# Larger first loads in a fused attention and Fourier-mix kernel: two head pairs in one transfer, and every engine's order made anew

## The chip, the cores and the metric

The kernel runs on one core of a Trainium2 chip. The metric is the device time of one execution in microseconds. The engines are TensorE (PE, with its weight loads PEld), VectorE (DVE), ScalarE (ACT), GpSimd (POOL) and SyncE (SP). DMA transfers are issued by SP and ACT on hardware queues, and by POOL on one software queue.

## The reference

Four batches, eight heads, 768 tokens, 64 values per head; d_model is 512. First a local attention with a linear distance bias, then a two-dimensional Fourier mix and a feed-forward part:

```python
scores = scale * np.matmul(q, k.transpose(0, 1, 3, 2))
keep = is_global | is_local          # 8 global keys, a band of 96
scores = np.where(keep, scores - slopes * dist, -1e9)
x = softmax(scores) @ v              # heads side by side: (4, 768, 512)
X = np.fft.fft(np.fft.fft(x, axis=1), axis=2)
u = x + np.real(X)
un = (u - mean(u)) / np.sqrt(var(u) + 1e-6)
out = u + np.maximum(un @ w_ch1, 0.0) @ w_ch2
```

All inputs and the output are float32; the kernel casts to float16 as it loads.

## The kernel before

Heads are taken in pairs (pair 0 holds heads 0 and 1, and so on to pair 3). The work is cut into units in four lists. In the unit names below, the number counts along the list.

- A, attention. For a pair of the first two batches: a unit that transposes q and k on TensorE (line 599), three score units (lines 676 and 690, with the exponential on ScalarE at line 713) and the products with v (line 769). Batch 0: A0 and A1 transpose pair 0, A2 to A4 are its scores, A5 transposes pair 2, A6 pair 1, A7 to A9 are scores of pair 2, A12 to A14 of pair 1, A15 transposes pair 3, A18 to A20 are its scores; A10 and A11, A16 and A17, A21 and A22, A23 and A24 are the two halves of the products with v of pairs 0, 2, 1 and 3. Batch 1: A25, A26, A30 and A34 transpose its pairs, A27 to A29, A31 to A33 and so on are scores, A41 to A44 products with v.
- M, the mix. Batch 0: M0 and M1 fold the output of pairs 1 and 3 on TensorE (line 960; pairs 0 and 2 are folded on VectorE, lines 913 to 945), M2, M3, M9 and M10 are the first transform (line 1052), M4 to M6 spread x (line 1113), M7, M8 and M13 the second transform (line 1140), M11, M12 and M14 transpose the centred rows.
- H, the first feed-forward product (line 1287), eight units for each of twelve chunks of 256 rows.
- G, the second feed-forward product (lines 1320 and 1429).

Every unit leaves follow-up operations for the other engines, named unit.number: the copy of transposed q and k out of PSUM (line 623 on VectorE, line 626 on ScalarE), the copy of a part of the transposed keys (lines 630 and 631; the scores need it), the exponentials, the normalization (lines 779 and 781), and so on. Loads, table work and the copies of v (lines 740 and 742; the products with v need them) have names that begin with T.

The order on each engine is written out by hand in the table `ORDER` of the class `Plan`: five lists of such names, one for each engine. The code only replays them (`run`, `unit_start`, `op_start`, `op_go`); engines wait for each other by semaphores. The constants in `op_go` and `move` are a cost model of the transfers; they choose among operations that are ready and free buffers, while each engine's own order is the list's. POOL's list holds its transfers among its copies, so a copy stands behind the transfers ahead of it. A software transfer takes one of eight lanes (`self.soft`), and must wait until the transfer that holds the lane has landed.

The loads of batch 0: pair 0's q and k come as four float32 transfers on the hardware queues (line 515) and are cast by ScalarE and VectorE. For pairs 1 to 3, POOL issues one transfer for q and one for k of each pair (line 539), and two for each pair's v (line 482; 64 partitions each). The table of distances for the scores (`misc<-distm`, line 1554) is also issued by POOL, behind q and k of pairs 2 and 3. Batch 1 already loads some pairs together: `n == 4` in `load_qk` (line 530) takes q of two pairs in one transfer, and `load_v` takes v by four heads (line 476).

Of the kernel before, what the change touches and what calls it, by code (L numbers as in the profile page):

```python
# [17 lines left out]
class Ring(str):  # L18

    k = 0  # L20
    n = 1
# [3 lines left out]
class Plan:  # L25
# [85 lines left out]
    def op_go(self, eng, name, start):  # L111
# [2 lines left out]
        fn()  # L114
        end = self.t[eng] = start + cost
        if dma:
            at = max(max(end + 0.55, 4.9) if eng == "POOL" else end + lat + 2.7 * (lat == 1.0 and end > 3.5), self.now)
            cell = [self.NEVER]
            self.q["SW" if eng == "POOL" else "AQ" if eng == "ACT" and at < 6.5 else "HW"].append([at, *dma, outs, uses, cell])
            lanes = self.lanes if nd > 0 else self.soft  # L120
            for _ in range(abs(nd)):
                lanes.append(cell)
                lanes.pop(0)
            if then is not None:
                self.tok[then] = end
            return
# [50 lines left out]
    def unit_start(self, unit):  # L177
# [7 lines left out]
        if not there:  # L185
# [6 lines left out]
    EQ = 4  # L192
    AQ = ()
    HW = (0,)
    U0 = 2
    PZ = 15
    EARLY = ("qk2", "qk1", "v0", "v2", "qk3", "v1", "v3")
    ORDER = {
# [9 lines left out]
        ),  # L208
        "ACT": (
# [9 lines left out]
        ),  # L219
        "DVE": (  # L220
# [11 lines left out]
        ),  # L232
        "POOL": (
# [5 lines left out]
        ),  # L239
        "SP": (  # L240
            "T.6 T.0 T.136 T.35 T.10 T.127 T.133 T.128 T.130 T.134 T.91 G7.1 G3.1 T.137 T.131 T.100 T.101 T.176 T.185 T.205 T.102 T.177 T.206 T.182 T.34 "
            "T.140 T.186 T.211 T.212 T.183 T.149 T.179 T.180 T.150 T.151 T.223 T.189 T.222 T.229 T.228 T.198 T.199 T.239 T.200 T.240 T.246 T.245 T.256 "
            "T.258 T.257 "
        ),
    }

# [60 lines left out]
def kernel(  # L307
# [85 lines left out]
    pl = Plan()  # L393
# [60 lines left out]
    stage = {}  # L454
# [10 lines left out]
    def load_v(b, hp):  # L465
        h0 = 2 * hp
        if b >= FB:
# [2 lines left out]
                                    v[b, h0:h0 + 2].rearrange("h (i m) d -> m (h i) d", m=P))  # L470
            swq(whole, 1.08, [("avdone", b - 2), ("wl", 7)], [("v", b, hp, t) for t in range(2)], (1536, 0.93), False)
            return
        if b == 1:
            for t in range(2 - hp % 2 * 2):
                def four(t=t):
                    nc.gpsimd.dma_start(v16[b % 2][64 * t:64 * t + 64, h0:h0 + 4, :, 0:Dh].rearrange("m h i d -> m (h i) d"),
                                        v[b, h0:h0 + 4].rearrange("h (i m t) d -> t m (h i) d", m=64, t=2)[t])
                swq(four, 1.08, [], [("v", b, hp, t), ("v", b, hp + 1, t)], (1536, 0.93))
            return
# [9 lines left out]
    def load_qk(b, hp):  # L489
# [3 lines left out]
        for w, src in enumerate((q, k)):  # L493
# [9 lines left out]
            def place():  # L503
                if (tag, ti) not in stage:
                    stage[tag, ti] = buf(tag, ti, [P, 2 if n < 6 else 1, 2, 2, NP, 2, Dh], FP16, 2 if n < 6 else 1)
                qk16[n] = stage[tag, ti][:, :, n % 2] if tag == "tt" else stage[tag, ti][:, n % 2 if n < 6 else 0]
            rows = src[b, h0:h0 + 2].rearrange("h s d -> (h s) d").rearrange("(m p t) d -> p m (t d)", p=P, t=2)
            if n in pl.HW:
                for h in range(2):
# [13 lines left out]
                             [("qk", n, w, h)], [("free", "u", w + n)], rank=0)  # L523
                continue

            if n == 4:
                def two(w=w, src=src):
                    place()
                    qk16[n + 1] = stage[tag, ti][:, :, 1]
# [1 line left out]
                                        src[b, h0:h0 + 4].rearrange("h s d -> (h s) d").rearrange("(m p t) d -> p m (t d)", p=P, t=2))  # L531
                swq(two, 1.08, free(tag, ti), [("qk", n, w), ("qk", n + 1, w)], (1536, 1.53))
                continue
            if n == 5:
                continue

            def run(w=w, rows=rows):
# [1192 lines left out]
```

## Time and profile before

| | |
|---|---|
| runs shown | 251.08, 251.26 (median), 252.32 us |
| profiled execution | 251.96 us, span of its instructions 250.2 us |
| mean granted TensorE clock | 0.986 |
| bytes | HBM read 31.48 MB, written 8.65 MB |

A row of busy time by stretches gives the stretch, then for each engine its busy time and number of instructions, the clock that was granted to TensorE (1.00 is full), the DMA share and the rate. A timeline row gives start, length, engine, line, operation, the tiles (out<-in), and in brackets how long the engine had been idle before it and what ended that. The sum of 1.76 us around the span belongs to the execution and not to any instruction.

### The profile page before, as it was taken

To read this page: it belongs to the slowest core of one execution; us is meant where nothing else is said; L and a number is where in the kernel's file an instruction comes from. 1 tells how busy PE (TensorE), PEld (TensorE's weight loads), DVE (VectorE), ACT (ScalarE), POOL (GpSimd) and SP (SyncE) were. 2 spreads that over 40 slices of the span, in tenths; PEclk is the share of its full clock that TensorE was granted. 3 is DMA by queue.
4 is the path that set the end of the run, shared out by engine and by line. 5 is a ranking of instruction groups with operands and counts; after the bars stand their busy time and mean duration, and the time that the engine had idled before them with its cause. 6 is when DMAs were issued, how large, how long until landed. Compare 5 with 4: busy or idle time off the path is not lost.

```text
span 250.2 us, 7615 instructions
## 1 busy us (share of the span) xinstructions
PE 235.1 (94%) x3251; PEld 193.0 (77%) x3251; DVE 199.0 (80%) x430; ACT 132.9 (53%) x222; POOL 111.1 (44%) x157
## 2 busy tenths in 40 slices
PE   7668799899999999999899999999999999999993
PEld 2446596778766667797788888899889888988882
DVE  1368999668988449999989999899996695676682
ACT  3038458886354698975276766825536353503300
POOL 8789928999570108997009412550004010300110
PEclk9979799999999999999999999999999999999999
DMA  7999999999999899999999780941913332032022
GB/s 156 204 139 135 213 195 203 186 125 177 163 135 196 208 190 86 193 133 107 252 240 244 48 107 5 156 35 35 245 61 125 47 105 65 1 86 84 3 84 84
DMA packets 96017, 32.88 MB, mean 131 GB/s; under 512 B 84304, under 2 KB 92624, under 8 KB 95984
## 3 DMA queue, kind: packets, MB, share of 16 engines
q0 software_dynamic: 66256, 17.39, 69.3%
q1 hardware_dynamic: 26416, 12.23, 24.4%
q10 hardware_dynamic: 3312, 2.79, 4.2%
q8 instruction: 25, 0.41, 0.7%
q14 instruction: 8, 0.07, 0.1%
HBM read 31.48 MB, written 8.65 MB: 160 GB/s over the span
## 4 chain that ended last, share of the span: by engine, by line
PE 79%; DMA 6%; DVE 6%; ACT 3%; POOL 2%; issue 1%; ACTq 0%; POOLq 0%
PE ph L1287 34%; PE pgD L1429 13%; PE pgA L1429 10%; PE pg L1320 6%; PE pav L769 4%; DMA misc<-distm 3%; PE py L1052 3%; DMA unT<-un 3%; PE pu L1140 3%; PE sc L684 3%; ACT ex L713 2%; PE sc L676 2%; POOL hT L539 1%; PE sc L690 1%; DVE qkT L623 1%
## 5 line engine op out<-in xcount | busy, mean ns | idle before, releaser
L1287 PE MATMUL ph<-unT,w 128*128 128x256 f16 x768 | 95.0, 273 | 1.0 <-DMA unT<-un 1.0
L1287 PEld LDWEIGHTS <-w 128*128 128x128 f16 x768 | 73.2, 98 | 12.3 <-DMA unT<-un 1.1
L1293 ACT ACTIVATE hT<-ph 128x512 f16<-128x512 f32 x74 | 43.3, 596 | 65.8 <-PE ph L1287 65.6
L1233 POOL TENSOR_SCALAR sm<-sm 128x2 f32<-128x2 f32 x12 | 4.0, 336 | 76.7 <-ACT un L1226 76.3
L1429 PEld LDWEIGHTS <-hT 128*128 128x128 f16 x320 | 30.8, 98 | 4.3 <-issue 0.4
L713 ACT ACTIVATE ex<-sc 128x1024 f16<-128x1024 f32 (+1 forms) x24 | 21.9, 957 | 13.8 <-PE sc L690 13.5
L710 ACT ACTIVATE er<-sc 128x1024 f16<-128x1024 f32 (+1 forms) x24 | 22.5, 952 | 10.2 <-PE sc L684 8.3
L1447 DVE SCALAR_TENSOR_TENSOR u<-pgA,sm,u 128x256 f32<-128x256 f32 (+1 forms) x30 | 17.1, 570 | 6.9 <-PE pgA L1429 6.6
L1294 DVE TENSOR_SCALAR hT<-ph 128x512 f16<-128x512 f32 x22 | 15.1, 688 | 6.7 <-PE ph L1287 6.5
L725 DVE TENSOR_TENSOR ex<-er,mk 128x1024 f16<-128x1024 f16 (+1 forms) x24 | 16.2, 686 | 4.4 <-ACT er L710 4.4
L1447 DVE SCALAR_TENSOR_TENSOR u<-pgD,sm,u 128x512 f32<-128x512 f32 (+1 forms) x21 | 15.2, 723 | 4.3 <-PE pgD L1429 4.0
L1320 PE MATMUL pg<-w,hT 128*128 128x512 f16 x64 | 15.8, 379 | 0.0
L769 PEld LDWEIGHTS <-ex 128*128 128x128 f16 x352 | 13.3, 99 | 2.1 <-issue 1.3
L1226 ACT ACTIVATE un<-un 128x512 f16<-128x512 f16 x24 | 14.9, 622 | 0.0
L1304 POOL DMA_INDIRECT out_dram<-u,back x4 | 4.7, 1184 | 22.3 <-DVE u L1447 22.0
L499 POOL DMA_DIRECT2D qk<-in_q_dram x16 | 13.3, 847 | 2.5 <-DMA w<-in_moe_w_ch_dram 1.4
L769 PE MATMUL pav<-v,ex 128*128 128x65 f16 x224 | 13.9, 196 | 0.1
L499 POOL DMA_DIRECT2D qk<-in_k_dram x16 | 13.4, 846 | 0.0
L676 PE MATMUL sc<-misc 64*64 64x512 f16 (+1 forms) x96 | 10.8, 422 | 2.8 <-DMA misc<-distm 1.2
L781 DVE TENSOR_TENSOR x<-pav,rc 128x384 f16<-128x384 f32 x24 | 12.6, 554 | 0.6
L1217 ACT ACTIVATE un<-u,sm 128x512 f16<-128x512 f32 x17 | 11.9, 714 | 1.7 <-DVE sm L1184 1.7
L623 DVE COPY qkT<-pt 128x1536 f16<-128x1536 f16 (+1 forms) x8 | 6.6, 850 | 6.8 <-PE pt L599 6.8
(170 smaller groups left out, 492.6 us busy)
## 6 DMA issues: line engine op xcount, KB each, us to landing
w<-in_moe_w_ch_dram POOLq DMA_DIRECT2D x8, 512.0 KB, 8.2
out_dram<-u SPq DMA_DIRECT2D x15, 256.0 KB, 2.5
v<-in_v_dram POOLq DMA_DIRECT2D x12, 192.0 KB, 5.8
qk<-in_q_dram POOLq DMA_DIRECT2D x16, 96.0 KB, 6.2
qk<-in_k_dram POOLq DMA_DIRECT2D x16, 96.0 KB, 5.0
xr<-xd SPq DMA_DIRECT2D x3, 512.0 KB, 4.3
xd<-x ACTq DMA_DIRECT2D x2, 768.0 KB, 4.4
v<-in_v_dram POOLq DMA_DIRECT2D x8, 96.0 KB, 7.6
```

The costliest lines, as they stand in the source:

```text
L499: nc.gpsimd.dma_start(qk16[n][:, w, :, h], src[b, h0 + h].rearrange("(i m) d -> m i d", m=P))
L676: nc.tensor.matmul(o, sid[r, 2 * hp + s, r], m, start=True, stop=False, skip_group_check=True, tile_position=(64 * s, 64 * t))
L710: A(mine(), cut(pa), AF.Exp, 0.0, 0.125)
L713: A(cut(expst[hp][:, :, g * 512:g * 512 + (384 if g == 2 else 512)]), cut(pa), AF.Exp, 0.0, 0.125)
L725: VT(o, mine(), m, op=ALU.mult)
L769: nc.tensor.matmul(o[:, s * 65:(s + 1) * 65], lhsT, w, start=(a == 0), stop=(a == len(ops) - 1), skip_group_check=True)
L1287: nc.tensor.matmul(ph[:, a * CH:(a + 1) * CH].rearrange("p (x m) -> p x m", x=2), W1[0][:, d, jb * P:(jb + 1) * P], UNT[c][:, :, d, :], st ...
L1293: pl.later([("ACT", act(512), lambda: A(dst, ph, AF.Relu)), ("DVE", dve(512), lambda: V.tensor_scalar_max(dst, ph, 0.0))], [], e, [("h", c ...
L1294: ("DVE", dve(512), lambda: V.tensor_scalar_max(dst, ph, 0.0))],
L1320: nc.tensor.matmul(pg, HT[c][:, jb, t * P:(t + 1) * P], W2[0][:, jb, :], start=(jb == 0), stop=(jb == NJ - 1))
L1429: nc.tensor.matmul(o, lhs(j), rhs(j), start=(first and j == 0), stop=(j == NK - 1), skip_group_check=True)
L1447: V.scalar_tensor_tensor(o, x, r(t), acc, op0=ALU.mult, op1=ALU.add)
```

## The change

Batch 0's pairs 2 and 3 are loaded together: q of four heads in one transfer, k of four heads in another, and v by four heads in two transfers instead of four. POOL issues 10 loads for batch 0's q, k and v instead of 14. The constant that the cost model gives for the start of the first software transfer goes from 4.9 to 5.5, and the lists of all engines are other ones.

```diff
-            at = max(max(end + 0.55, 4.9) if eng == "POOL" else end + lat + 2.7 * (lat == 1.0 and end > 3.5), self.now)
+            at = max(max(end + 0.55, 5.5) if eng == "POOL" else end + lat + 2.7 * (lat == 1.0 and end > 3.5), self.now)
...
     HW = (0,)
+    PAIRS = (2, 3)
...
-        if b == 1:
+        if b == 1 or hp in pl.PAIRS:
             for t in range(2 - hp % 2 * 2):
...
-                qk16[n] = stage[tag, ti][:, :, n % 2] if tag == "tt" else stage[tag, ti][:, n % 2 if n < 6 else 0]
+                qk16[n] = stage[tag, ti][:, :, n % 2] if n in (4, 5) or n in pl.PAIRS else stage[tag, ti][:, n % 2 if n < 6 else 0]
...
-            if n == 4:
+            if n in (4,) + pl.PAIRS[:1]:
...
-            if n == 5:
+            if n in (5,) + pl.PAIRS[1:]:
                 continue
```

The lists, by what differs at their heads (before, then after; the T numbers shift, since there are fewer loads):

```diff
 PE
-A0 A5 A1 A15 A3 A2 A4 A7 A20 A6 A9 A8 A10 A19 A11 A12 A14 A30 A16 A13 A17 A18 A21 A22 A37 A36 A23 M0 A24 A25 A34 M1 M4 A35 A26 A28 A38 M5 M2
-A29 A39 M3 M9 A32 M7 A40 M8 A31 M10 M6 A27 M11 M13 H0 A33 H1 A43 H2
+A0 A1 A3 A5 A15 A2 A6 A9 A4 A7 A8 A10 A18 A11 A14 A16 A12 A13 A17 A30 A20 A21 A19 A22 A25 A26 A23 A34 A24 A37 M0 M1 A38 A35 M5 A36 A39 M2 M3
+A28 M4 M7 A29 M8 M9 M6 M11 M10 A27 A40 H0 A33 A32 H1 M13 H2 A31 H3
...
 ACT (its two or three transfers first; A1.1, A1.2, A15.1, A6.1 are copies out of q and k)
-T.2 T.8 T.4 T.7 T.1 T.5 A3.0 A4.0 A2.0 A7.0 A20.0 A8.0 A19.0 A9.0 A14.0
+T.0 T.4 T.9 T.1 T.5 A1.1 A1.2 A3.0 A15.1 A2.0 A6.1 A4.0 A9.0 A8.0 A7.0 A14.0
...
 DVE (A6.0 is pair 1's key copy, T.66 before and T.62 after pair 0's copy of v)
-T.53 T.51 T.3 A1.1 A1.2 T.49 A5.1 A15.1 T.52 A15.0 T.66 A6.1 T.50 A6.0 A10.0 A11.0 T.68
+T.7 T.45 T.3 T.47 A5.1 A6.0 T.62 T.48 T.46 T.64 A10.0 A11.0 T.66
...
 POOL (A1.0 and A5.0 are key copies of pairs 0 and 2; T.9 before is the distance table, T.26 after is q of batch 1's third pair)
-T.11 T.12 T.19 T.20 T.9 T.14 T.15 T.16 T.18 T.13 T.17 T.21 T.22 A1.0
+T.11 T.12 T.13 T.14 T.15 T.18 T.16 T.17 T.26 A1.0 T.21 T.20 A5.0
```

In the new lists the distance table (T.9) is the third transfer that ScalarE issues; the identity goes to SyncE. From the fourth chunk on the lists of all engines differ in many places by one to three entries.

More of the change, by code (lines that the diff above doesn't have):

```diff
@@ L199 @@
         "PE": (
[8 rows of a table removed]
[8 rows of a table added]
         ),
         "ACT": (
[9 rows of a table removed]
[9 rows of a table added]
         ),
         "DVE": (
[11 rows of a table removed]
[11 rows of a table added]
         ),
         "POOL": (
[5 rows of a table removed]
[5 rows of a table added]
         ),
         "SP": (
-            "T.6 T.0 T.136 T.35 T.10 T.127 T.133 T.128 T.130 T.134 T.91 G7.1 G3.1 T.137 T.131 T.100 T.101 T.176 T.185 T.205 T.102 T.177 T.206 T.182 T.34 "
-            "T.140 T.186 T.211 T.212 T.183 T.149 T.179 T.180 T.150 T.151 T.223 T.189 T.222 T.229 T.228 T.198 T.199 T.239 T.200 T.240 T.246 T.245 T.256 "
-            "T.258 T.257 "
+            "T.8 T.6 T.2 T.129 T.123 T.31 T.132 T.124 T.126 T.130 T.87 T.133 T.10 T.127 G7.1 G3.1 T.96 T.97 T.172 T.98 T.173 T.30 T.181 T.178 T.201 T.136 "
+            "T.202 T.182 T.208 T.207 T.175 T.179 T.145 T.176 T.146 T.218 T.147 T.224 T.219 T.185 T.194 T.225 T.195 T.196 T.242 T.236 T.235 T.241 T.252 "
+            "T.254 T.253 "
         ),
```

66 rows, old and new, of the table ORDER are left out of this document.

## The prediction

> **What bounds the kernel now.** I read the page first, then busy time by stretches, then the timelines of single engines in the first 55 us, at last the chain that ended last.
>
> ```profile
> span 250.2 us, 7615 instructions
> PE 235.1 (94%) x3251; PEld 193.0 (77%) x3251; DVE 199.0 (80%) x430; ACT 132.9 (53%) x222; POOL 111.1 (44%) x157
> ...
> 0.00:20.00 20.00, 13.80 (x211) 8.52 (x212) 7.74 (x19) 6.49 (x9) 16.23 (x29) 0.91 1.72 167
> 20.00:40.00 20.00, 17.51 (x427) 14.44 (x427) 18.92 (x51) 13.06 (x18) 14.82 (x22) 0.91 1.55 186
> 40.00:60.00 20.00, 19.00 (x381) 14.73 (x374) 15.77 (x38) 16.75 (x28) 19.01 (x31) 1.00 1.45 168
> ...
> 100.00:120.00 20.00, 18.65 (x332) 15.49 (x330) 19.76 (x42) 14.77 (x25) 17.08 (x21) 1.00 1.92 148
> ...
> 15.00:20.00 5.00, 4.73 (x118) 3.73 (x119) 2.30 (x4) 3.63 (x5) 4.94 (x11) 0.67 2.41 141
> 25.00:30.00 5.00, 3.24 (x77) 2.64 (x74) 4.85 (x12) 2.92 (x3) 4.80 (x8) 0.85 1.69 213
> 30.00:35.00 5.00, 5.00 (x116) 4.30 (x115) 4.44 (x20) 2.27 (x5) 3.01 (x5) 0.81 1.45 184
> ```
>
> Columns: the stretch, busy PE, PEld, DVE, ACT, POOL with counts, granted clock, DMA share, GB/s. PE is idle for 15.1 us of the span: 6.2 in the first 20 us, 2.5 in the next, 1.0 up to 60, 1.35 between 100 and 120, the rest in the tail. So from the first feed-forward product on PE is the bound, and time can come only from the 9.7 us idle before it, from 1.35 us later, and from the reduced clock: busy time times (1 - clock) is 1.6, 0.5 and 0.95 us in the last three rows, 3.0 in all. From 20 to 40 us DVE is busy for 18.92 of 20: there DVE carries the chain, and PE fills.
>
> The first load waits, on POOL, PE and ACT:
>
> ```profile
> 8.49 0.75 POOL L482 DMA_DIRECT2D v<-in_v_dram  x1 [0.77 <-DMA hT<-in_q_dram]
> 9.58 0.83 POOL L539 DMA_DIRECT2D hT<-in_q_dram  x1 [0.34 <-DMA hT<-in_k_dram]
> 10.68 0.75 POOL L482 DMA_DIRECT2D v<-in_v_dram  x1 [0.28 <-DMA hT<-in_q_dram]
> 11.76 0.74 POOL L482 DMA_DIRECT2D v<-in_v_dram  x1 [0.33 <-DMA hT<-in_k_dram]
> 13.36 0.74 POOL L482 DMA_DIRECT2D v<-in_v_dram  x1 [0.86 <-DMA misc<-distm]
> 14.10 0.71 POOL L630 COPY mk<-qkT 128x512 f16<-128x512 f16 x1
> 14.87 0.29 POOL L631 COPY mk<-qkT 128x128 f16<-128x128 f16 x1
> 15.21 0.31 PE L690 MATMUL sc<-qkT,mk 64*64 64x128 f16 x2 [1.54 <-POOL mk L631]
> 9.34 1.63 PE L599 MATMUL pt<-ident,hT 128*64 128x128 f16 x36 [0.56 <-DMA hT<-in_k_dram]
> L626 ACT ACTIVATE qkT<-pt 128x1536 f16<-128x1536 f16 x1 | 1.4, 1444 | 0.0
> L713 ACT ACTIVATE ex<-sc 128x1024 f16<-128x1024 f32 x16 | 16.1, 1024 | 11.3 <-PE sc L690 11.0
> ```
>
> POOL has eight loads under way; the ninth waits until the first has landed. The releases 8.49, 9.58, 10.68, 11.76 are q2, k2, q3, k3 of the first batch: 1.09 us for 192 KB, and 13.36 the distance table, 1.60 us. Pair 0's scores wait for its key copy on POOL, at 14.10.
>
> **The change, part by part.** *Loads.* q2 and q3 become one transfer, k2 and k3 another. The queue moves a load in 1.09 us however many wait, so merging saves no queue time: the merged q lands when k2 did, 9.4, the merged k when k3 did, 11.7. Pair 2 loses 1.1 us on q and 2.2 on k. The table leaves POOL's queue for ACT's, where it runs beside these loads: that costs them 0 to 1.6 us (its price in the old queue); I take 1.1, since the hardware queue moves it at the same time as the other: q at 10.5, k at 12.8. Later loads come 1.6 less 1.1 earlier. POOL issues four loads fewer (0.75 to 0.83 each), and four of the rest carry twice the bytes; it waits for landings there, so this is worth nothing by itself.
>
> The Trainium skill (DMA: Bandwidth & Descriptors, Anatomy of one DMA) gives each such transfer about 2.0 us of fixed time besides its bytes. By that, four transfers fewer would save 8 us. The spacing of 1.09 us shows that in this queue the fixed part lies under the neighbours, and the trace decides.
>
> *First score.* The new order has eight loads, then the ninth (q of batch 1's third pair), then pair 0's key copy. So POOL waits to 10.5, issues (0.83), copies (1.05 from the rows at 14.10 and 14.87): the first score starts at 12.4, not 15.21. The transposes of pair 0 end by 8, so PE idles from 8 to 12.4 and begins at half clock. Score, pair 2's and pair 3's transposes (24 each; 36 took 1.63 at full clock) then take about 0.9, 1.4 and 1.2: 15.9. Before, the same five units were done at 16.0. Nothing is won yet.
>
> *Copies out.* Four copies of transposed q and k go from DVE to ACT. ACT, in order: pair 3's copy from 15.9 (1.44), an exponential (1.02), pair 1's copy (1.44): 19.8. DVE's next entry is pair 1's key copy, which waits for that; then comes pair 0's v copy. So DVE starts its long stretch at 20.5, and not at 15.85:
>
> ```profile
> 15.85 0.53 DVE L740 COPY vB<-v 128x528 f16<-128x528 f16 x1 [0.99 <-DMA v<-in_v_dram]
> ...
> 19.60 0.96 DVE L623 COPY qkT<-pt 128x1536 f16<-128x1536 f16 x1 [1.80 <-PE pt L599]
> ...
> 20.80 0.82 DVE L630 COPY mk<-qkT 128x512 f16<-128x512 f16 x1
> 21.66 0.50 DVE L631 COPY mk<-qkT 128x128 f16<-128x128 f16 x1
> 22.32 0.20 DVE L779 RECIPROCAL rc<-pav 128x6 f32<-128x6 f32 x1 [0.17 <-PE pav L769]
> ...
> 29.42 0.28 DVE L630 COPY mk<-qkT 128x512 f16<-128x512 f16 x1
> ...
> 34.53 0.20 DVE L779 RECIPROCAL rc<-pav 128x6 f32<-128x6 f32 x1 [0.42 <-PE pav L769]
> ...
> 35.24 0.68 DVE L965 CAST zy<-pf 128x512 f16<-128x512 f32 x1
> ...
> 44.18 0.68 DVE L1068 CAST zy<-py 128x512 f16<-128x512 f32 x1
> 47.48 0.69 DVE L1068 CAST zy<-py 128x512 f16<-128x512 f32 x1 [1.69 <-ACT zy L1066]
> ...
> 53.36 1.03 PE L1287 MATMUL ph<-unT,w 128*128 128x256 f16 x8
> ```
>
> Before, DVE goes from 15.85 to 44.18, when the fold is done: 28.3 us. In the new order this stretch loses the idle 1.80, 0.17 and 0.42, one copy out (0.96), a key copy (1.3 of 20.80 to 22.16), another (0.55 at 29.42) and a cast (0.68): 5.9. It gains a key copy (0.55) and two scalings (0.4). So 23.4 us from 20.5: 43.9, 0.3 earlier. This supposes that PE always has the next piece ready.
>
> *From the fold to the first feed-forward product, H0.* 9.2 us now. DVE's wait of 1.69 at 47.48 goes, since that cast now stands behind the sums of M7; two casts come to DVE (0.69, and one of 128x1024, about 1.2 from 0.69 for half of it); the transposes M11 stand right behind M6 instead of after A27. I follow the new order: M3 and its casts 46, M7 47.3, its sums 49.1, centring on ACT 50.7, M11 51.2, copied out 51.9. H0 starts at 51.95, 1.4 earlier.
>
> *What PE still owes at H0.* A31, A32 and M13 stood ahead of H0 and come after it now:
>
> ```profile
> 49.67 0.41 PE L676 MATMUL sc<-misc 64*64 64x512 f16 x4
> 50.24 0.39 PE L1052 MATMUL py<-t,ww 128*128 128x256 f16 x2
> 52.46 1.00 PE pu L1140 x16
> ```
>
> A score is 0.57 (start to next start), M13 1.0: 2.1 us. As PE is full from there, they are paid in full: -1.4 + 2.1 = +0.7.
>
> *Later.* One stall can go:
>
> ```profile
> PE ph L1287 <- DMA unT<-un: 1.0, 1, 1.0
> 112.29 7.66 DMA unT<-un
> 32.34 1.79 PE pf L960 x32
> ```
>
> The centring that this transpose waits for stands two H units earlier in the new order. That is worth 0 to 1.35 us (all idle of 100 to 120), if nothing takes its place; I take 0.4, nearer to nothing, because the whole later order is new too. The tail keeps its order on PE.
>
> The sum is +0.3 us. The profiled execution took 251.96 with a span of 250.2; it would be 252.3. Against the median shown, 251.26, which is 0.7 lower, that is 251.6.
>
> **The rivals.** *The clock (slower).* M0 needs both halves of pair 1's output. DVE now puts the second half behind two copies out, at about 35.3, while PE has done what stands before by 32.5. PE is idle for 2.8 us and may fall to half clock just when the two folds (1.79 us each) carry the chain; DVE's fold stands waiting for M1, and so do all after it. The rows at 25 and 30 us show such a drop after a stretch only 3.24 of 5 busy. At half clock for some 3.2 us the folds end 1.6 us later. It decides once M1's last copy comes after 40.2, where DVE needs it; it would be there at 39.9, so nearly all is paid: +1.4, and 0.3 for waits behind it: 253.3. Against it: PE's gap may be shorter, if DVE is behind.
>
> The Trainium skill (TensorE: Matmul & The Clock Gate, Part 1) states that the clock halves after an idle window of about 3.4 us. By that alone 2.8 us would not do it; the trace shows 0.85 and 0.81 after windows far from idle, so it speaks for the rival.
>
> *Early data (faster).* If the table disturbs nothing, q lands at 9.4 and k at 11.7: scores, copies on ACT, and DVE's stretch all begin 1.1 earlier, DVE is the chain throughout, and the stall at 119 goes wholly (0.95 beyond my share): 249.5. For it: DVE's later stretch has no idle left to swallow the lead. Against: ACT's three pieces in a row stay.
>
> *Doing nothing new.* The merge itself changes no bytes; if DVE's load is what counts, the time stays. That is my forecast's own case.
>
> *Another wait (slower).* Some place in 200 us of new order waits 1 to 3 us more, as the one at 119 does now: up to 254.6.
>
> **How the numbers follow.** The forecast has 0.35, with a range of its own from 250.3 to 252.5; the clock 0.30, early data 0.27, another wait 0.08. Measured runs spread by 0.5%, and 0.5% (1.26 us) is about what can be told from no change. Faster 0.27, same 0.35, slower 0.38. Eight times in ten: from 248.8 (early data, and another 0.7 from the reduced clock) to 254.6.
>
> **What would show it.** Right: the first release of POOL's ninth load at 10 to 11; first key copy at 11.4; clock 0.50 around 12 to 16; DVE's first v copy near 20.5; H0 near 52. Wrong: H0 before 50.7 or after 53, PE idle of over 1 us behind 60 in a new place, or DVE with idle time between 21 and 44.

## The result, and the profile after

| | before | after |
|---|---|---|
| median of the runs | 251.5 us (251.08 to 252.32, 6 runs) | 255.43 us (253.22 to 257.05, 6 runs) |
| ratio | | 1.0132, 95% interval 1.0095 to 1.0169 |
| profiled execution | 251.96, span 250.2 | 255.45, span 253.4 |
| mean granted clock | 0.986 | 0.987 |

The change costs 1.3% where no change was forecast, and the time lies above the range given (248.8 to 254.6). The comparisons leave disturbed runs out, so a ratio can differ a little from that of the medians, here and below. Line numbers after the change are one higher than before, for everything that the prediction quotes.

The page after, its busy time, and busy time by stretches; the last row is from the first feed-forward product (H0) to the end:

```profile
span 253.4 us, 7599 instructions
PE 235.7 (93%) x3251; PEld 193.9 (77%) x3251; DVE 200.9 (79%) x432; ACT 132.8 (52%) x221; POOL 107.9 (43%) x151
...
0.00:20.00 20.00, 13.77 (x195) 8.63 (x196) 2.81 (x8) 8.53 (x10) 13.93 (x26) 0.91 1.86 167
20.00:40.00 20.00, 16.38 (x392) 13.78 (x393) 17.97 (x52) 11.82 (x16) 17.78 (x25) 0.91 1.86 178
40.00:60.00 20.00, 18.50 (x380) 13.94 (x380) 17.36 (x43) 17.52 (x30) 16.48 (x22) 1.00 1.62 188
60.00:80.00 20.00, 19.08 (x257) 13.97 (x254) 17.99 (x37) 7.58 (x15) 7.56 (x9) 1.00 1.75 164
...
100.00:120.00 20.00, 19.30 (x316) 16.47 (x314) 19.73 (x37) 13.64 (x23) 19.39 (x26) 1.00 1.67 125
120.00:140.00 20.00, 19.17 (x237) 16.57 (x234) 18.87 (x36) 11.55 (x22) 7.47 (x10) 1.00 1.18 213
53.24:253.40 200.16, 193.79 (x2412) 162.99 (x2404) 167.99 (x346) 101.02 (x182) 65.04 (x86) 1.00 0.81 117
```

The same last row, of the kernel before:

```profile
53.36:250.20 196.84, 191.44 (x2354) 161.14 (x2352) 161.95 (x339) 101.50 (x182) 67.60 (x88) 1.00 0.82 119
```

These two rows split the whole difference. H0 starts at 53.24 instead of 53.36: -0.12. Behind it PE works 193.79 instead of 191.44: +2.35. It idles 200.16 - 193.79 = 6.37 instead of 5.40: +0.97. Around the span stand 255.45 - 253.4 = 2.05 instead of 1.76: +0.29. The sum is 3.49, which is 255.45 - 251.96. The new order moves work behind H0 and gets nothing for it. PE, which before was full from 60 us on but for the stall at 120, now waits in two more rows there (19.08 and 19.17 of 20, where both had 20.00).

The timelines of POOL, DVE and PE, the rows that the prediction's steps name:

```profile
11.21 0.83 POOL L540 DMA_DIRECT2D qk<-in_q_dram  x1 [2.56 <-DMA hT<-in_q_dram]
12.03 0.63 POOL L631 COPY mk<-qkT 128x512 f16<-128x512 f16 x1
...
20.60 0.87 DVE L741 COPY vB<-v 128x528 f16<-128x528 f16 x1
24.77 0.20 DVE L780 RECIPROCAL rc<-pav 128x6 f32<-128x6 f32 x1 [0.28 <-PE pav L770]
28.93 0.20 DVE L780 RECIPROCAL rc<-pav 128x6 f32<-128x6 f32 x1 [0.61 <-PE pav L770]
38.49 0.28 DVE L938 SCALAR_TENSOR_TENSOR zy<-ww,eA 128x128 f16<-128x128 f16 x1
39.28 0.56 DVE L945 TENSOR_TENSOR xr<-zy 128x768 f16<-128x768 f16 x1 [0.51 <-ACT zy L966]
45.00 0.28 DVE L1028 TENSOR_TENSOR ww<-xr 128x256 f16<-128x256 f16 x1
...
13.06 0.32 PE L691 MATMUL sc<-qkT,mk 64*64 64x128 f16 x2 [0.86 <-POOL mk L632]
22.57 0.19 PE L770 MATMUL pav<-vB,ex 128*128 128x65 f16 x1 [1.38 <-DVE vB L743]
28.37 0.19 PE L770 MATMUL pav<-v,ex 128*128 128x65 f16 x1 [0.99 <-DVE x L782]
42.14 0.30 PE L691 MATMUL sc<-qkT 64*64 64x256 f16 x4 [0.78 <-issue]
47.39 1.05 PE L1141 MATMUL pu<-t,zy 128*128 128x128 f16 x16
51.23 0.42 PE L1258 MATMUL ptu<-ident,un 64*64 64x64 f16 x32
52.04 0.38 PE L1053 MATMUL py<-t,ww 128*128 128x256 f16 x2 [0.39 <-ACT zy L1067]
52.35 0.41 PE L677 MATMUL sc<-misc 64*64 64x512 f16 x4
52.81 0.33 PE L677 MATMUL sc<-misc 64*64 64x384 f16 x4
53.24 1.05 PE L1288 MATMUL ph<-unT,w 128*128 128x256 f16 x8
68.30 0.35 PE L1258 MATMUL ptu<-ident,un 64*64 64x64 f16 x20 [0.91 <-issue]
112.48 1.03 PE L1430 MATMUL pgA<-tt,sb 128*128 128x256 f16 x8 [0.65 <-DVE u L1448]
131.04 1.03 PE L1430 MATMUL pgA<-misc,hT 128*128 128x256 f16 x8 [0.83 <-DVE u L1448]
```

DVE's long stretch runs from 20.60 to 45.28. It stands idle three times in it, 1.40 us in all. Twice (0.28 and 0.61) it waits for a product of PE; PE in turn stands 1.38 and 0.99 us for DVE, so neither has the next piece ready for the other. The third wait, of 0.51, the view puts down to a copy of ACT, but it fits DVE's own result better: in all fourteen profiles with the new early lists, line 945 starts 0.51 or 0.52 us behind the end of line 938 on DVE, while the end of ACT's copy moves from 0.06 us ahead of that start to 0.71. In the order before, a copy out of q and k stands at this place:

```profile
36.43 0.29 DVE L937 SCALAR_TENSOR_TENSOR zy<-ww,eA 128x128 f16<-128x128 f16 x1
36.63 0.95 DVE L623 COPY qkT<-pt 128x1536 f16<-128x1536 f16 x1
37.50 0.55 DVE L944 TENSOR_TENSOR xr<-zy 128x768 f16<-128x768 f16 x1
```

Behind H0 there are new waits at 68, 112 and 131, while the one of 0.99 at 120 is gone (100 to 120: 0.70 idle instead of 1.35). Two waits, at 42.14 and 68.30, say "issue": PE was idle, and nothing that the view knows released it. These issue waits became a question of their own.

### The profile page after: what moved, and what is told of

It is laid out like the page before. It is cut to its first block, busy times and chain, and to the rows that moved or that the text cites. A ratio compares the mean times of both kernels' runs of the same rounds, so it can differ in the third digit from the quotient of the medians.

```text
span 253.4 us, 7599 instructions
## 1 busy us (share of the span) xinstructions
PE 235.7 (93%) x3251; PEld 193.9 (77%) x3251; DVE 200.9 (79%) x432; ACT 132.8 (52%) x221; POOL 107.9 (43%) x151
## 3 DMA queue, kind: packets, MB, share of 16 engines
q1 hardware_dynamic: 26560, 12.26, 23.4%
## 4 chain that ended last, share of the span: by engine, by line
PE 62%; POOL 12%; DVE 11%; DMA 6%; ACT 4%; issue 4%; POOLq 0%; ACTq 0%
PE ph L1288 24%; PE pgD L1430 11%; PE pgA L1430 8%; DMA hT<-in_q_dram 4%; PE pg L1321 4%; PE py L1053 4%; POOL qk L500 3%; PE pav L770 3%; POOL v L470 2%; DMA v<-in_v_dram 2%; PE pu L1141 2%; POOL vB L741 2%; DVE u L1448 2%; PE sc L685 1%; PE sc L691 1%
## 5 line engine op out<-in xcount | busy, mean ns | idle before, releaser
L1288 PE MATMUL ph<-unT,w 128*128 128x256 f16 x768 | 93.6, 273 | 0.0
L1294 ACT ACTIVATE hT<-ph 128x512 f16<-128x512 f32 x69 | 40.7, 595 | 67.5 <-PE ph L1288 67.2
L1295 DVE TENSOR_SCALAR hT<-ph 128x512 f16<-128x512 f32 x27 | 18.3, 687 | 13.3 <-PE ph L1288 13.2
L711 ACT ACTIVATE er<-sc 128x1024 f16<-128x1024 f32 (+1 forms) x24 | 22.5, 951 | 9.2 <-PE sc L685 7.6
L835 POOL DMA_INDIRECT xr<-xd,back x3 | 3.4, 1124 | 29.5 <-DVE hT L1295 19.7
L726 DVE TENSOR_TENSOR ex<-er,mk 128x1024 f16<-128x1024 f16 (+1 forms) x24 | 14.9, 638 | 0.0
L1218 ACT ACTIVATE un<-u,sm 128x512 f16<-128x512 f32 x18 | 12.8, 718 | 3.6 <-DVE sm L1185 3.5
L770 PE MATMUL pav<-vB,ex 128*128 128x65 f16 x128 | 10.9, 196 | 1.4 <-DVE vB L743 1.4
```

The lines of the kernel that those rows point to most:

```text
L711: A(mine(), cut(pa), AF.Exp, 0.0, 0.125)
L726: VT(o, mine(), m, op=ALU.mult)
L770: nc.tensor.matmul(o[:, s * 65:(s + 1) * 65], lhsT, w, start=(a == 0), stop=(a == len(ops) - 1), skip_group_check=True)
L1288: nc.tensor.matmul(ph[:, a * CH:(a + 1) * CH].rearrange("p (x m) -> p x m", x=2), W1[0][:, d, jb * P:(jb + 1) * P], UNT[c][:, :, d, :], st ...
L1294: pl.later([("ACT", act(512), lambda: A(dst, ph, AF.Relu)), ("DVE", dve(512), lambda: V.tensor_scalar_max(dst, ph, 0.0))], [], e, [("h", c ...
L1295: ("DVE", dve(512), lambda: V.tensor_scalar_max(dst, ph, 0.0))],
```

## Experiments

Medians, with the range and the kernel before on the same chip; the ratio is that of the comparison, with its 95% interval.

| kernel | median us | before | ratio |
|---|---|---|---|
| loads merged, old order | 253.65 (252.18 to 255.64) | 251.97 | 1.0073 (1.0037 to 1.0110) |
| new order, loads apart | 259.18 (258.35 to 260.05) | 251.97 | 1.0291 (1.0251 to 1.0331) |
| new order up to H8, then old | 265.23 (264.77 to 267.35) | 251.97 | 1.0558 (1.0511 to 1.0604) |
| old order up to H8, then new | 257.75 (255.56 to 258.35) | 251.97 | 1.0224 (1.0176 to 1.0273) |
| after, v copied first | 254.77 (253.81 to 258.03) | 251.62 | 1.0187 (1.0119 to 1.0254) |
| after, late adds first | 254.9 (253.59 to 257.1) | 251.62 | 1.0151 (1.0087 to 1.0214) |
| after, +90 instructions | 254.43 (253.48 to 257.05) | 251.62 | 1.0140 (1.0077 to 1.0204) |
| before, centring earlier | 251.63 (250.11 to 252.51) | 251.62 | 1.0010 (0.9975 to 1.0045) |
| after, v first and adds first | 255.83 (253.91 to 256.64) | 251.44 | 1.0177 (1.0129 to 1.0226) |
| after, these two and +90 | 254.7 (251.62 to 256.91) | 251.44 | 1.0079 (1.0037 to 1.0122) |
| after, transfers held back | 256.28 (255.76 to 259.02) | 251.44 | 1.0219 (1.0166 to 1.0271) |
| before, +90 instructions | 252.34 (250.27 to 254.04) | 252.31 | 0.9991 (0.9960 to 1.0021) |
| loads merged, old order, +90 | 252.59 (251.53 to 255.25) | 252.31 | 1.0040 (1.0002 to 1.0077) |
| after, +30 instructions | 255.55 (254.43 to 256.43) | 252.31 | 1.0124 (1.0093 to 1.0155) |
| after, +210 instructions | 256.43 (253.43 to 259.23) | 252.31 | 1.0121 (1.0076 to 1.0166) |

### The loads and the order apart

The merge alone: the new loads under the lists of before, where the T entries of the loads that fell away are left out.

```diff
+    PAIRS = (2, 3)
-            "T.11 T.12 T.19 T.20 T.9 T.14 T.15 T.16 T.18 T.13 T.17 T.21 T.22 A1.0 ...
+            "T.11 T.12 T.9 T.14 T.15 T.16 T.18 T.13 T.17 T.19 T.20 A1.0 ...
```

> Before's order on every engine, with the loads of pairs 2 and 3 merged (four entries of POOL's list fall away, nothing else). Theory 'order' (the loss comes from the new lists, the merge itself costs next to nothing): 251 to 252.5 us; k of pairs 2 and 3 lands at 11.5 as k3 did, so A5, second in PE's list, waits 2.2 us longer, but pair 0's key copy on POOL still sets the first score near 15. Theory 'merge' (pair 2 and pair 0's v come too late in larger transfers, whatever the order): 253.5 to 256, H0 at 55 or later.

POOL's timeline of this kernel gives the landings, the table still in this queue:

```profile
9.58 0.96 POOL L477 DMA_DIRECT2D v<-in_v_dram  x1 [1.34 <-DMA hT<-in_q_dram]
11.74 0.74 POOL L483 DMA_DIRECT2D v<-in_v_dram  x1 [1.21 <-DMA hT<-in_k_dram]
```

Merged q lands when k of pair 2 did before (9.58), and merged k when k of pair 3 did (11.74 against 11.76): the merge buys no queue time. PE waits for the later data of pair 2 (1.5 and 1.6 us for q and k), H0 moves to 56.51, and the wait at 120 shrinks to 0.29. The median, 253.65, lies where the theory "merge" had it, and H0 behind 55 is its sign. So in the old order the merge isn't free: it costs 0.4 to 1.1%. In its profile PE also has 3.3 us of issue waits.

The order alone: the new lists over the old loads, each merged transfer written as two (the head of POOL's list).

```diff
-            "T.11 T.12 T.19 T.20 T.9 T.14 ...
+            "T.11 T.12 T.19 T.20 T.13 T.14 T.15 T.18 T.24 T.16 T.17 T.23 T.30 A1.0 ...
```

> After's order on every engine, with the loads of pairs 2 and 3 separate again, each pair of loads at the place of the merged one. Theory 'order': 254.5 to 256, like the changed kernel, with DVE's first v copy at 20 to 21. Theory 'merge': 251 to 252.5, with the first v copy more than 1.5 us earlier.

```profile
9.66 0.75 POOL L482 DMA_DIRECT2D v<-in_v_dram  x1 [1.70 <-DMA hT<-in_q_dram]
14.55 0.83 POOL L539 DMA_DIRECT2D qk<-in_q_dram  x1 [0.49 <-DMA hT<-in_q_dram]
15.37 0.62 POOL L630 COPY mk<-qkT 128x512 f16<-128x512 f16 x1
```

Both theories missed. POOL now issues five loads ahead of pair 0's key copy that each wait for an earlier one to land, so the first score comes at 16.4 and H0 at 56.72. This order needs the merge. The row also prices the table on the other queue: q lands at 9.66 instead of 8.49, 1.17 us. In the changed kernel merged q lands at 11.21, against 9.58 with the merge alone, 1.63 later; the lists differ there too.

Half of each order, joined at H8:

> Merged loads; after's lists up to H8 (about 68 us), then before's. Theory 'the loss is made before H8' (1.9 us by H0: 0.1 us won in time, 2.05 of work still owed; 0.9 more in the wait inside M14 at 68 us): 253.8 to 255. Theory 'it is made later' (waits of 0.65 and 0.83 us at 112 and 131 in place of one of 1.35): 251 to 252.5.

> Separate loads; before's lists up to H8, then after's. Theory 'the loss is made before H8': 251 to 252.3. Theory 'it is made later': 253 to 255.

The first joint makes a wait of 10.16 us of its own (PE for DVE's add, at 98.68), so it tells nothing of the lists. The second makes one of 2.84 at 69.00; its span of 254.7 less the 3.5 that PE idles between 60 and 80 is 251.2, about 1 above before. So most of the loss belongs to the early lists; the size is argued from a subtraction, not shown.

### The named waits

One entry moved on DVE, so that it doesn't stand idle 3.95 us ahead of the key copy:

```diff
-            "T.7 T.45 T.3 T.47 A5.1 A6.0 T.62 T.48 T.46 T.64 A10.0
+            "T.7 T.45 T.3 T.47 A5.1 T.62 T.48 T.46 A6.0 T.64 A10.0
```

> The changed kernel (profiled span 253.4), with one move on VectorE: pair 0's copy of v (and the two scalings behind it) ahead of pair 1's key copy, for which VectorE now stands idle 3.95 us. Early theory (the loss is made before the first feed-forward product: DVE's long stretch starts too late): the products with v of pair 0 start some 1.5 to 2.5 us earlier than 22.6, PE's wait of 1.38 there goes, H0 comes at 51 to 52 rather than 53.24, and the end moves by as much: 253.0 to 254.2. Later theory (the new waits behind 60 us make the loss, and PE's own pieces hold DVE in the stretch): H0 moves by less than 0.5 and the time stays at 255 to 255.8. Fetch rival: PE reaches the boundary of its next instruction packet earlier than the packet, so its issue wait near 42 us grows from 0.78 to 2 or more and eats the gain.

The waits of PE in this kernel (engine, line waited for, us in total, times, longest):

```profile
PE pt L600 <- DVE qkT L624: 2.4, 2, 1.2
PE sc L691 <- issue: 0.6, 1, 0.6
PE ptu L1258 <- issue: 0.6, 1, 0.6
```

The wait of 1.38 is gone, DVE copies v at 18.45 instead of 20.60, and H0 comes at 52.11, 1.13 earlier; the span is 251.9, 1.5 less. That is the early theory by its profile. Half of DVE's lead of 2.15 is lost again: pair 1's key copy (20.04 to 20.98) now stands inside the stretch, and the three longest idle times in it are 0.30, 0.61 and 0.51, as much as before. So this edit starts the stretch earlier and doesn't remove its idle time. PE waits 2.4 for DVE's copies out instead of 1.0. The runs don't confirm a gain: the median is 0.7 us lower, but the ratio, 1.0187, is not below the 1.0132 of the changed kernel.

Two moves behind 100 us:

```diff
-A60.0 A50.1 M17.8 T.198 G16.0 M20.0
+A60.0 G16.0 A50.1 M17.8 T.198 M20.0
-T.138 T.139 G22.0 G23.0 T.140
+T.138 G22.0 G23.0 T.139 T.140
```

> The changed kernel, with two moves on VectorE late in the list: the add of pgA that PE waits for at 112.48 (0.65 us) ahead of a multiplication, a centring and a sum, and at 131.04 (0.83 us) the adds of pgD and pgA ahead of two steps of the fold. Later theory: both waits go or shrink below 0.3 each, 0.8 to 1.5 us less, 254.0 to 254.6. Early theory: PE has no other slack behind 60 us, so it expects the same of these two and nothing of the rest; H0 stays at 53.2. Rival (waits move on): the pieces put back (a centring, a sum, a fold step) become late, PE waits as long in new places, time 255.2 to 256.

The two waits are gone, 0.25 and 0.51 come in their place at 113.14 and 107.60, and PE idles 0.93 us behind 60 instead of 2.45. But H0 is at 55.20, though nothing ahead of it was edited: the issue wait at 42 is now 1.83, and the granted clock is 0.50 from 42.8 to 46.2, where the first profile had 1.00. The gain is real behind 60 and hidden by what one execution does ahead of it.

The kernel before, without its stall at 120:

```diff
-M17.7 H29.0 M17.3 M17.8 H28.0
+M17.7 M17.8 H29.0 M17.3 H28.0
```

> The kernel before, with one move on ScalarE: the second centring of chunk 4 (111.56) ahead of an activation and a square, so that the transposing transfer can start 1.2 to 1.5 us earlier than 112.29. Theory (PE is full from H0 on and every wait removed there is time): the wait of 0.99 at 120.00 goes, nothing replaces it, 250.6 to 251.2 against 251.6 to 252. Rival: the activation that is put back, or the transfer's own queue, takes its place: 251.5 to 252.3.

The wait of 0.99 is gone (100 to 120: 19.64 busy instead of 18.65), the span is 249.6, 0.6 less, and the median is the same within 0.4%. A profile can lose a wait that the median doesn't notice.

### PE's own instructions

The profile's page shows a queue for instructions (packets, MB, share of 16 engines); each of its packets is 16 KB:

```profile
q8 instruction: 25, 0.41, 0.7%
```

25 packets for 3251 PE and 3251 PEld instructions is one for about 260. In the trace, counting those instructions, the issue waits fall on the 1219th and the 2243rd, which are 4 x 256 and 8 x 256 behind the 195th; the issue waits of the kernels below fall on the same series. The packet that the wait at 42.14 needs starts at 38.93 and takes 1.50 us; PE passed the boundary before it at 34.85. So it seems that PE asks for a packet when it enters the one before it, and here got through 256 instructions in less time than the packet took to come. Two things are left open: PE goes on 1.71 us after the packet's end, and behind 80 us a packet can start before PE reaches the boundary (82.17, boundary at 84.77). The DMA queues in the 4.05 us up to 38.9, and in the 1.6 us behind it (packets, MB, and the sum of the packets' times as a share of 16 engines, over 100% where packets overlap):

```profile
q0 software_dynamic: 2758, 0.73, 232.0%
...
q0 software_dynamic: 1617, 0.20, 368.3%
q8 instruction: 1, 0.02, 5.9%
```

In the first stretch there is no packet of instructions, and the software transfers move 0.73 MB. To see whether the place is PE's count, the warm-up was cut finer:

```diff
-            nc.tensor.matmul(pz[:, 0, :], EG[:, 0, 0:P], EG[:, 0], start=True, stop=True)
+            for i in range(4):
+                nc.tensor.matmul(pz[:, 0, 128 * i:128 * i + 128], EG[:, 0, 0:P], EG[:, 0, 128 * i:128 * i + 128], start=True, stop=True)
```

> The changed kernel, with the 15 warm-up products of 512 columns cut into 60 of 128: the same columns, and 90 instructions more on PE (weight loads and products) before the first transpose. Fetch theory (the issue waits of 0.78 at 42.14 and 0.91 at 68.30 are PE waiting for its next packet of 256 instructions): both waits leave their instructions (a score of the second batch, a transpose of the centred rows), and waits without a releaser can come only 90 instructions earlier, at about 38.6 (0 to 1.2 us) and 66.6 (0 to 0.5). Time 254 to 255.8. Rival (the score and the transpose wait for a buffer or a write that the profile doesn't show): the same two instructions wait as long, 0.7 to 1.0 each, and the time stays.

```profile
59.60 0.60 PE L1288 MATMUL ph<-unT,w 128*128 128x256 f16 x4 [0.88 <-issue]
```

Both waits left their instructions, and the only one is on an H product, where the 1987th instruction now is. The waits are PE's packets. The places forecast (38.6 and 66.6) were wrong; another boundary got the wait.

Whether the transfers under way delay a packet: a 512 KB load and a 96 KB one were moved behind that of 44.48.

```diff
-T.22 T.61 T.63 ... T.56 T.54 T.102 T.51 ... T.52 T.115
+T.22 T.63 ... T.56 T.54 T.51 ... T.52 T.61 T.102 T.115
```

> The changed kernel, with two software transfers (a 512 KB part of the second weights, issued at 24.64, and a 96 KB one of k, at 35.42) moved on POOL's queue behind the load of 44.48, so that 608 KB less are under way from 31 to 44 us. Theory (PE's packets of instructions wait for the engines of the software transfers): the packet that PE asks for at 34.85 and gets at 38.93 to 40.43 comes 1 us or more earlier and the issue wait at 42.14 (0.78) goes; a later packet may be late instead. Time 254.0 to 255.4. Rival (the delay of a packet has nothing to do with these transfers): the issue wait at 42 stays between 0.5 and 1.9. Second rival: the transfers moved are missed later (a wait for w or for k of batch 2), time above 256.

```profile
PE pgA L1430 <- DVE u L1448: 1.9, 2, 1.6
PE sc L691 <- DVE mk L632: 1.3, 1, 1.3
PE pav L770 <- POOL vB L743: 1.1, 1, 1.1
```

The three packets of 30 to 45 us started 0.9, 2.4 and 1.9 us after PE passed the boundary, instead of 2.9, 4.1 and 3.7, and no issue wait is left. In three other profiles with the same boundaries (the changed kernel again, v copied first, late adds first) it was 2.1 to 3.3, 3.8 to 4.9 and 3.7 to 3.9. So fewer bytes under way bring the packet sooner. It gained nothing: PE waits at other places (the rows above), it seems for what the moved loads bring, and the time is the second rival's.

The three edits together, first the two of DVE, then with the finer warm-up:

> The changed kernel with both edits on VectorE: pair 0's copy of v ahead of pair 1's key copy, and the adds of 112 and 131 us ahead of what stood before them. Theory (the loss is a sum of named waits on a full PE): H0 at 52.1 as with the first edit, the two waits of 0.65 and 0.83 gone as with the second, the issue waits near 41 and 67 still there (0.6 to 1.8 and 0 to 0.9): span 250.4 to 251.2, time 252.4 to 253.6. Rival (each removed wait is paid again elsewhere): 254.3 to 255.5 as with either edit alone.

```profile
PE sc L691 <- issue: 2.5, 1, 2.5
PE pt L600 <- issue: 1.5, 2, 0.9
PE ptu L1258 <- issue: 0.6, 1, 0.6
PE pav L770 <- issue: 0.5, 1, 0.5
```

> As after_two, and with the warm-up in 60 products of 128 columns, 90 instructions more on PE before the first transpose. Theory (sum of named waits): the issue waits leave the instructions at 41 and 67, but may come at others (0.9 at about 59 before): span 250 to 251, time 252 to 253.2, still not below the kernel before, since 2.1 us of work stand behind H0 that stood ahead of it. Rival (each removed wait is paid again): 254 to 255.5.

Without the shift, 5.1 us of issue waits ate what the two edits freed: H0 is at 53.93 in a profile of 254.42 us, and the median, 255.83, is even above the rival's range. With it they are 0.8 us, PE idles 0.54 and 0.12 in the rows of 100 and 120, H0 is at 52.76, the span 250.6: the sum of the named waits, as forecast. But the median is 254.7, in the rival's range, and only the profile agrees with the theory. The ratio of 1.0079 is the lowest of the edited kernels, and its interval overlaps that of the changed kernel.

Is it chance where the packets end?

> The kernel before, with the 15 warm-up products of 512 columns cut into 60 of 128 (same columns, 90 instructions more on PE). It showed no issue wait behind 2 us. Pace theory (in the order of before PE passes 256 instructions slowly enough, and its packets come early enough, wherever they end): issue waits stay below 0.5 us in sum, time 251.2 to 252.2. Chance theory (before was lucky in where its packets end): issue waits of 1 us or more in sum, time 252.5 to 254.

> The loads merged under the order of before, with 90 instructions more in the warm-up. Without them PE had issue waits of 1.4, 1.2, 0.5 and 0.3 us between 21 and 43 us and took 253.65. Pace theory (larger transfers delay the packets, wherever they end): the waits move to other instructions, 1.5 to 3.5 us in sum, time 253 to 254.5. Chance theory: they fall below 1 us in sum, time 251.5 to 252.6.

> The changed kernel, with the warm-up in 30 products of 256 columns (30 instructions more on PE). Pace theory: issue waits of 0.8 to 3 us in sum in the first 75 us, 30 instructions ahead of the two places of the changed kernel or others, time 254.3 to 255.8. Chance theory: another place of the packets' ends frees PE of them, below 0.5 in sum, time 252.8 to 253.8.

> The changed kernel, with the warm-up in 120 products of 64 columns (210 instructions more on PE, nearly one packet). Pace theory: issue waits of 0.8 to 3 us in sum in the first 75 us, time 254.3 to 255.8. Chance theory: below 0.5 us in sum, time 252.8 to 253.8. Third possibility: the weight loads of 64-column products set the warm-up's pace, it ends later and the first transposes with it: everything 1 us or more later, first score past 14.

The waits, of before with 90 instructions more:

```profile
PE pf L960 <- issue: 1.5, 1, 1.5
PE sc L690 <- issue: 0.5, 1, 0.5
```

The place is chance in both kernels: the old order gets 2.0 us of such waits, the merged loads lose theirs (3.3 down to 0.2), and 30 instructions more give the changed kernel 3.3. But the cost isn't: with its 2.0 us the kernel before has H0 at 54.63 instead of 53.36, the idle time between 100 and 120 falls from 1.35 to 0.36, and the time is 0.9991 of before. In this profile it has slack there that swallows an early delay. The merged loads come to 1.0040 without these waits. The changed kernel keeps 1.2 to 1.4% with each of the three shifts. (The profiled execution with 210 took 258.23 us, 1.8 above the median, and isn't read here.)

What differs between two executions of one program:

> The changed kernel once more, unedited, to compare two executions of one program (the first: 255.45 us, issue waits of 0.78 at 42.14 and 0.91 at 68.30, H0 at 53.24). Packet theory (the time varies because the packets of PE's instructions and the first loads come at other times in each execution): first score, issue waits and H0 differ by 0.5 to 2 us, and the end by what H0 and the later issue waits differ; the waits for DVE at 112 and 131 us are the same within 0.1. Rival (the variation is spread over the whole execution, such as by the clock): H0 within 0.5 us, and the difference of the ends made behind it.

> The kernel with all three edits once more (the first profile: 252.53 us, issue waits of 0.8, H0 at 52; other runs went from 251.6 to 256.9). Packet theory: where this execution is 2 us or more longer, issue waits and the idle time of PE ahead of 70 us are longer by as much; where it is within 1 us, they are the same within 1 us. Rival: the difference is made behind 70 us.

> A third execution of the kernel with all three edits, with the same expectation: packet theory, the difference of the ends to the other two is made ahead of 70 us, in issue waits and first loads; rival, behind 70 us.

The changed kernel again: 255.6 us, span 253.5, H0 at 53.51, issue waits of 0.6 and 0.7, the waits for DVE's adds 0.3 us longer in sum. With three edits: 253.47 and 253.03 (252.53 the first time), H0 at 53.50 and 53.57 (52.76), spans 251.5 and 251.1 (250.6): the ends differ by 0.9 and 0.5 from the first, H0 by 0.74 and 0.81, so the difference is made ahead of H0. But PE's packets don't make it: the issue waits are 0.8 the first time, none in the second profile and 0.6 in the third. The first score comes 0.33 and 0.60 later (12.85 and 13.12 against 12.52), and the mean granted clock is 0.986 and 0.985 instead of 0.993; these two causes were not separated. By five profiles the edits bring 2.0 to 3.1 us, and 2.0 to 2.6 without the one at 0.993. None of the five caught one of the runs of 255 to 257 that the edited kernel also has. What those do differently is open; the mean clock doesn't tell, since seven of the twelve runs have 0.993 and take 251.62 to 256.4.

## Why the prediction was wrong

The prediction's sum gave 252.3 for the profiled execution, and 255.45 was measured. By its own steps:

- *The queue and the merge.* Right in kind, small in size: merged q lands with pair 2's k, as forecast, but with the table on the other queue it lands 1.63 later than with the merge alone (1.17 in the order alone), and 1.1 was taken. POOL's ninth load came at 11.21 against 10.5, outside the 10 to 11 named as a sign, and the first score at 13.06 against 12.4.
- *DVE's stretch starts at 20.5.* It started at 20.60, partly by luck: the first score was 0.7 late, and the steps from it to DVE's copy of v took 7.5 us instead of 8.1. The stretch's work, 23.4 us, was right: 24.68 less 1.40 idle is 23.3.
- *"This supposes that PE always has the next piece ready."* This failed. The fold ended at 45.28, not 43.9, by the 1.40 us in which DVE stood idle. For 0.89 of it PE's piece wasn't ready. The other 0.51 is most likely DVE's own result: the sum took out the copy of 36.63 with its full 0.96, though it had covered this wait, so that only some 0.45 could be saved (an estimate from the two rows). No run took the idle time alone away.
- *From the fold to H0.* The sum was right by luck: 7.96 us where 8.05 were forecast. From the fold's end to M7 (47.39) it took 2.11 and not 3.4, since the products before M7 start at 44.01, while the fold still runs; so at M7 the lateness of the fold was made up. To M11 (51.23) it took 3.84 instead of 3.9. The last piece failed: H0 was put 0.75 behind M11, right after the copy out, but in the new list M10, A27 and A40 stand between them (the rows at 52.04, 52.35 and 52.81), and it took 2.01. It is 2.01 in twelve of fourteen profiles with the new early lists and more in the other two, and 1.34 in all six with the old ones. So H0 missed 51.95 by 1.38 - 1.29 - 0.06 + 1.26 = 1.29.
- *What PE still owes.* Right, and a little small: 2.35 instead of 2.1. PE is full behind H0 but for the waits named, so the time is paid. This price is read from the rows; no run put A31, A32 and M13 back ahead of H0.
- *Later, -0.4.* This failed too, by as much as H0: +0.97. The stall at 120 did go (0.65 less in its row), but 0.92 came at 68 and 0.83 at 131. The first is a packet of instructions, of which the prediction knew nothing; the second is DVE's order, an add behind two steps of the fold.
- *Around the span.* 0.29 more, not foreseen and not explained.

Together 1.29 + 0.25 + 1.37 + 0.29 = 3.2 above the forecast, which with its own +0.3 is 3.5.

Of the rivals, the clock did not come: it was reduced at 12.5 to 16 (forecast) and at 22.5 to 26.5, and full at the folds from 36.29 on, as the busy time by stretches shows. DVE's wait of 0.28 for PE lies in the second of these stretches; whether the clock made it was not tested.

```profile
12.50:16.00 3.50, 2.94 (x60) 2.77 (x62) 0.83 (x1) 1.03 (x1) 1.79 (x4) 0.52 3.18 141
22.50:26.50 4.00, 3.81 (x61) 2.80 (x64) 3.54 (x13) 1.72 (x3) 3.94 (x6) 0.57 1.72 171
26.50:40.00 13.50, 11.55 (x308) 10.29 (x302) 12.10 (x36) 7.60 (x10) 11.34 (x17) 1.00 2.02 197
```

Early data did not come: q landed at 11.21, not at 9.4. "Another wait", with 0.08, was the nearest, and it was several: its end of 254.6 counted one. Of the signs named for a wrong forecast two came: H0 after 53, and DVE idle between 21 and 44. The new places behind 60 stayed below 1 us each (0.92 and 0.83), so they were sought too coarsely.

## What to carry to other kernels

A chain through two engines that feed each other costs the work of the one plus every place where it waits for the other: sum up one engine's instructions only as a lower bound, and look for the pieces that the other must hand back. A copy that stands between an instruction and the one that needs its result may cover a wait, and taking it out then saves less than its length. When a milestone is forecast, read every engine's list to its end: three units between M11 and H0 were left out here, and an error of that size the other way hid that the fold was late as well. Work pushed behind the point from which an engine is full is paid, so a milestone that comes no later can still mean a slower kernel. And a wait removed in one profile is worth something only where nothing downstream has slack and the median moves: three edits here gained 2 to 3 us in profiles and 0.7 us in the median.

## What the runs showed of the hardware

PE's instructions come in packets of 16 KB, one for each 256 instructions. Ahead of the two issue waits of the changed kernel the packet started 4.1 and 4.2 us after PE had passed the boundary before it, beside software transfers (0.73 MB in the stretch shown), and PE went on 1.7 and 1.4 us after the packet's end. In that kernel and its variants PE stood for up to 2.5 us at a time, and up to 5.1 us in one execution. The wait shows as "issue", at any instruction; 90 instructions more in the warm-up move it.

The Trainium skill (Runtime: NRT & Kernel Launch, Instruction fetch mechanics) describes blocks of 16 KiB and 256 instructions, and has their cost mostly hidden. The size agrees with the 25 packets and 0.41 MB of the profile; the hiding doesn't hold here, by the 0.78 and 0.91 us of the changed kernel and the rows of the kernel with two edits.
